# Hourglass attention and a gated FFN: pair 0's q, k and v by the hardware queues, and a new written order of the fill

## The chip, the cores and the metric

One core of a Trainium2 chip. The metric is the device time of one launch in microseconds; less is better. The core has TensorE (PE in the profile, with its weight loads as PEld), VectorE (DVE), ScalarE (ACT), GpSimd (POOL) and SyncE (SP). Each works through its own instructions strictly in the order in which they are written; DMAs are issued by SP, ACT and GpSimd.

## The reference

```python
q, k, v: (8, 8, 576, 64)          # batch, heads, positions, head width
# coarse attention on means of 4 neighbouring positions
q_d, k_d, v_d = (t.reshape(B, H, 144, 4, D).mean(axis=3) for t in (q, k, v))
out_up = repeat(softmax_attention(q_d, k_d, v_d), 4, axis=2)
# local attention: |i - j| < 4
scores = where(abs(i - j) < 4, q @ k.T / 8, -1e9)
attn_out = out_up + softmax(scores) @ v
x = attn_out.transpose(0, 2, 1, 3).reshape(4608, 512)
out = (maximum(x @ w_gate, 0) * (x @ w_val)) @ w_out       # 512 -> 1536 -> 512
```

Inputs and output are fp32; the kernel works in fp16 with fp32 sums.

## The kernel before, in words

The 64 heads are taken as 32 pairs of heads; four pairs make a batch row of 576 tokens. The FFN runs over 9 chunks of 512 tokens (`TCH`), each of 12 blocks of 128 hidden columns (`hg` products with w_gate, `hv` with w_val), and a chunk needs xT of all four pairs of its tokens. Attention runs some pairs ahead of the FFN.

Steps of a pair, with the names that the written order uses: `loadq`, `loadk`, `loadv` load q, k and v and cast them to fp16 on the way (GpSimd's queue, L328 and L358). For the first nine pairs PE turns q and k over (`tr`, L388, three groups of eight products), and `ev` copies the result from PSUM (L402), by ACT or VectorE as a letter says, the full columns to qkT and the sums of four to qkd. `s1` are the scores of both attentions (L451, L462), `ex` and `ed` their exp on ACT (L472, L486), `ma` the band mask on VectorE (L478), `vd` and `vc` the pooled v (L432, L441). For pairs 0 to 3 `su` and `sd` are the products with v (L511, L499), `ru`, `rd`, `tu`, `td` divide on VectorE, and `xp` and `xe` bring the result to xT (L646, L658). Later pairs use `den` and `num`, `ln`, `inv`, `xn` and `xsum`, and from pair 8 on the steps `scores`, `exp`, `mask`, `o`, `ln`, `xn`, `xsum` of the repeating part. From pair 9 on q and k come in halves of one head each (L333), and SP turns both over by a transposing DMA (`flip`, L368), after which VectorE pools them (`pool`, L375). From pair 11 on v is also loaded a second time (`v4`, L363), and GpSimd adds it up to vd (`v2`, L410, and `v1`, L416).

The weights come in slices: `wg`, `wv` and `wo`, four of 384 KB each, all by GpSimd's queue. The products with w_out (`p`, L748) are made in seven instead of eight parts, from sums that VectorE prepares (`wt`, L714, `next`, `sum`, L742), and SP writes the output (L698) from four y buffers.

Buffers: seven for q and k of a pair (`qk16`, pair modulo 7), seven for v, four for qkT, three for vd. A load into a buffer waits for the last reader of what was in it; for q and k of pairs 9 on that is the transposing DMA.

The order of everything is written out. The three strings are `FRONT` (the fill), `ORDER` (the repeating part) and `MAIN` (the end); each engine receives its own steps in the order of the string. A token as `qk/b2/0@1` is the third of four half loads for pair 4*1 + 2*0 + 4 + 1 + 4 = 13. In `FRONT`, `warm` and `brief` are dummy products on zeros (L833, L843), `pads` and `ones` constants that are written into buffers. Before the string the kernel issues constants and q of pair 0, which alone comes in fp32 by SP's queue and is cast by ACT (`cast`), sets constants on VectorE and runs 14 wide dummy products. GpSimd's loads carry, in the builds of both kernels, eight semaphores in turn: each waits until the load eight before it is complete.

Of the kernel before, what the change touches and what calls it, by code (L numbers as in the profile page):

```python
# [9 lines left out]
FP32 = mybir.dt.float32  # L10
# [8 lines left out]
pads loadk/0 loadv/0 loadq/1 loadk/1 loadv/1 loadq/2 cast tr/0/2/4 loadk/2 ev/0/20V/4 tr/0/1/3  # L19
tr/0/0/2 ev/0/21V/4 ev/0/10A/3 vd/0/6 loadv/2 ev/0/11A/3 ev/0/01A/2 ev/0/00A/2 loadq/3 warm/5/6  # L20
tr/1/0/7 vc/0/6 s1/0/2 ev/1/00A/7 loadk/3 tr/1/2/1 ed/0/2 tr/1/1/0 ev/1/20V/1 ev/1/11A/0 loadv/3
sd/0/6 ev/1/21V/1 ev/1/10A/0 rd/0/6 ex/0/0/2 td/0/6 wg/0 brief/16/2 vd/1/6 ev/1/01A/7 warm/2/7 ma/0/0
ex/0/1/2 s1/1/0 wv/0 ma/0/1 ed/1/0 ones/4 su/0/4 ex/1/1/0 ru/0/4 loadq/4 ex/1/0/0 tu/0/0/4
warm/5/7 tr/2/1/2 tr/2/2/3 tu/0/1/4 ev/2/11A/2 tr/2/0/0 ev/2/10A/2 loadk/4 ev/2/21V/3 xp/0/0/4 ev/2/20V/3
ev/2/01A/0 xp/0/1/5 ev/2/00A/0 ma/1/0 loadv/4 vc/1/6 warm/1/7 s1/2/0 ma/1/1 xe/0/0A/4 xe/0/1V/5 sd/1/6
ex/2/1/0 ones/5 su/1/4 rd/1/6 td/1/6 ed/2/0 ru/1/4 warm/3/7 vd/2/6 loadq/5 tu/1/1/4 ex/2/0/0 tr/3/1/2
tu/1/0/4 tr/3/2/3 loadk/5 vc/2/6 tr/3/0/0 ev/3/20V/3 ev/3/10A/2 xp/1/1/5 sd/2/6 ev/3/21V/3
loadv/5 ev/3/01A/0 xe/1/1V/5 xp/1/0/4 ev/3/00A/0 ma/2/0 ev/3/11A/2 ma/2/1 xe/1/0A/4 s1/3/0 wg/1
rd/2/6 su/2/4 td/2/6 ed/3/0 ru/2/4 ex/3/0/0 tu/2/1/4 hv/0/0/7 wv/1 hv/0/1/7 tu/2/0/4 ex/3/1/0
vd/3/6 ma/3/0 ones/6 warm/4/1 xp/2/1/5 vc/3/6 xp/2/0/4 ma/3/1 sd/3/6 xe/2/1V/5 xe/2/0A/4 loadq/6 tr/4/0/0  # L30
rd/3/6 su/3/4 td/3/6 tr/4/1/2 loadk/6 ru/3/4 hv/1/0/1 ev/4/11A/2 tu/3/0/4 hg/0/0/6 ev/4/10A/2
hg/0/1/6 tu/3/1/4 loadv/6 tr/4/2/3 ev/4/01A/0 ev/4/00A/0 xp/3/1/5 ev/4/21V/3 ev/4/20V/3 xp/3/0/4
wg/2 hv/0/2/7 xe/3/1V/5 xe/3/0A/4 hg/1/0/0 s1/4/2 wv/2 hv/0/3/7 ex/4/0/2 hv/1/1/1 loadq/7
hg/1/1/0 hg/1/2/0 ed/4/2 ma/4/0 hv/1/2/1 hg/0/2/6 hg/0/3/6 ex/4/1/2 hg/1/3/0 hv/1/3/1 relu/0/6
tr/5/0/2 ma/4/1 tr/5/1/3 loadk/7 relu/1/0 tr/5/2/4 den/4/1/5 ev/5/20V/4 vd/4/6 ev/5/10A/3
hg/3/*/0 ev/5/21V/4 gate/0/7 vc/4/6 ev/5/00A/2 gate/1/1 hg/2/*/6 ev/5/11A/3 loadv/7 ev/5/01A/2
relu/3/0 den/4/0/4 relu/2/6 hv/2/*/7 wg/3 ln/4 num/4/0/2 wv/3 gate/2/7 tr/6/1/0 inv vd/5/1
num/4/1/3 loadq/8 s1/5/4 vc/5/1 xn/2 hv/3/*/1 ex/5/0/4 ev/6/11V/0 ed/5/4 ma/5/0 hg/4/*/2
gate/3/1 ex/5/1/4 loadk/8 tr/6/0/4 relu/4/2 ma/5/1 tr/6/2/1 hg/5/*/6 ev/6/20V/1 ev/6/00A/4
ev/6/01V/4 ev/6/10A/0 ev/6/21V/1 den/5/0/4 xsum/4 wo/0 den/5/1/5 num/5/0/2 ln/4 hv/4/*/3 wo/1  # L40
inv hv/5/*/7 gate/4/3 wo/2 relu/5/6 hg/6/*/0 gate/5/7 qk/b0/0@0 num/5/1/3 relu/6/0 vd/6/1 xn/2
s1/6/4 vc/6/1 tr/7/1/0 ex/6/1/4 hv/6/*/1 ed/6/4 qk/b1/0@0 ma/6/1 hg/7/*/2 ex/6/0/4 hg/8/*/6
ma/6/0 relu/7/2 gate/6/1 qk/b2/0@0 tr/7/0/4 num/6/0/2 ev/7/01V/4 ev/7/00A/4 den/6/1/5 tr/7/2/1
qk/b3/0@0 ev/7/10A/0 den/6/0/4 ev/7/20V/1 hv/7/*/3 relu/8/6 ev/7/21V/1 xsum/5 wo/3 ln/4 hv/8/*/7
gate/7/3 inv vd/7/1 ev/7/11V/0 gate/8/7 num/6/1/3 vc/7/1 hg/9/*/0 loadv/8 xn/2 s1/7/4 relu/9/0
xsum/6 hg/10/*/2 ex/7/0/4 wt/0 v/b/0@0 ex/7/1/4 hv/10/*/3 ma/7/0 relu/10/2 ma/7/1 hv/9/*/1
ed/7/4 gate/10/3 qk/a0/1@0 hg/11/*/0 gate/9/1 qk/a1/1@0 next/0/1@0 den/7/0/4 relu/11/0 tr/8/1/2
qk/a2/1@0 den/7/1/5 flip/9 ev/8/11V/2 tr/8/2/3 ev/8/10A/2 next/1/1@0 tr/8/0/0 qk/a3/1@0
hv/11/*/1 ln/4 ev/8/01V/0 ev/8/20V/3 v/a/1@0 ev/8/21V/3 inv num/7/0/6 gate/11/1 num/7/1/7
p/1/0@1 qk/b0/1@0 ev/8/00A/0 sumhi/0/0@1 xn/6 p/2/0@1 keep/1/0@1 qk/b1/1@0 vd/8/1 xsum/7  # L50
scores/a/0@1 vc/8/1 qk/b2/1@0 sumhi/1/0@1 wt/1 vd/9/1 exp/a1/0@1 hg/0/0@1 qk/b3/1@0 ed/a/0@1
c11//0@1 v/b/1@0 sum/2/0@1 p/6/0@1 vc/9/1 relu/0/0@1 wt/2 p/5/0@1 v4/b/1@0 exp/a0/0@1 flip/10
hv/0/0@1 mask/a1/0@1 keep/2/0@1 qk/a0/0@1 mask/a0/0@1 p/7/0@1 gate/0/0@1 o/a00/0@1 sum/3/0@1
keep/3/0@1 o/a01/0@1 qk/a1/0@1 o/a10/0@1 ln/a0/0@1 o/a11/0@1 c22//0@1 hg/2/0@1 wt/3 qk/a2/0@1
ln/a1/0@1 p/3/0@1 qk/a3/0@1 pool/b/0@1 inv/a/0@1 p/4/0@1 v/a/0@1 hv/2/0@1 c21//0@1 c12//0@1
v4/a/0@1 relu/2/0@1 xn/a0/0@1 hg/1/0@1 xn/a1/0@1 hv/1/0@1 relu/1/0@1 qk/b0/0@1 flip/11
xsum/a/0@1 scores/b/0@1 gate/1/0@1 hg/3/0@1 exp/b1/0@1 qk/b1/0@1 next/0/0@1 exp/b0/0@1 qk/b2/0@1
hg/4/0@1 mask/b1/0@1 ed/b/0@1 mask/b0/0@1 qk/b3/0@1 hv/3/0@1 next/1/0@1 relu/3/0@1 gate/2/0@1
v2/b/0@1 relu/4/0@1 o/b00/0@1 o/b01/0@1 gate/3/0@1 o/b10/0@1 ln/b0/0@1 o/b11/0@1 vd/10/0
pool/a/0@1 v/b/0@1 p/1/1@1 ln/b1/0@1 hg/5/0@1 v4/b/0@1 inv/b/0@1 flip/12 hv/5/0@1 qk/a0/1@1  # L60
keep/1/1@1 xn/b1/0@1 qk/a1/1@1 p/6/1@1 xn/b0/0@1 hv/4/0@1 qk/a2/1@1 keep/2/1@1 next/2/0@1
vc/10/0 qk/a3/1@1 scores/a/1@1 relu/5/0@1 gate/4/0@1 p/7/1@1 v/a/1@1 exp/a0/1@1 gate/5/0@1
p/2/1@1 exp/a1/1@1 mask/a0/1@1 v4/a/1@1 hg/0/1@1 ed/a/1@1 mask/a1/1@1 xsum/b/0@1 keep/3/1@1
qk/b0/1@1 o/a00/1@1 relu/0/1@1 o/a01/1@1 c11//1@1 o/a10/1@1 o/a11/1@1 next/3/0@1 flip/13 p/4/1@1
ln/a1/1@1 qk/b1/1@1 pool/b/1@1 p/5/1@1 ln/a0/1@1 v2/a/1@1 hg/2/1@1 inv/a/1@1 c22//1@1 hv/0/1@1
c21//1@1 v1/a/1@1 xn/a0/1@1 hg/1/1@1 v2/b/1@1 xn/a1/1@1 p/3/1@1 relu/1/1@1 gate/0/1@1 qk/b2/1@1
scores/b/1@1 c12//1@1 hg/3/1@1 qk/b3/1@1 exp/b1/1@1 xsum/a/1@1 exp/b0/1@1 flip/14 mask/b1/1@1
qk/a0/0@2 hv/1/1@1 ed/b/1@1 mask/b0/1@1 qk/a1/0@2 hv/2/1@1 gate/1/1@1 relu/3/1@1 v4/a/0@2
pool/a/1@1 relu/2/1@1 o/b00/1@1 o/b01/1@1 o/b10/1@1 v1/b/1@1 ln/b0/1@1 o/b11/1@1 hv/3/1@1
v/b/1@1 ln/b1/1@1 hg/5/1@1 gate/3/1@1 qk/a2/0@2 inv/b/1@1 gate/2/1@1 hg/4/1@1 v1/a/0@2 xn/b1/1@1  # L70
hv/4/1@1 v4/b/1@1 relu/4/1@1 xn/b0/1@1 relu/5/1@1 qk/a3/0@2 hv/5/1@1 xsum/b/1@1 qk/b0/0@2
qk/b1/0@2 qk/b2/0@2 qk/b3/0@2 v/a/0@2
"""
MAIN = """
o:v2/a/0@6 fl/31 o:v1/b/0@6 o:v2/b/0@6 o:scores/a/0@6 o:gate/5/1@5 o:p/1/0@6 o:exp/a0/0@6 o:gate/4/1@5
o:hg/0/0@6 o:exp/a1/0@6 o:sumhi/0/0@6 o:ed/a/0@6 o:mask/a0/0@6 o:p/2/0@6 o:mask/a1/0@6 o:relu/0/0@6
o:sumhi/1/0@6 o:next/0/1@5 o:o/a10/0@6 o:keep/1/0@6 o:o/a00/0@6 o:o/a01/0@6 o:next/1/1@5 o:o/a11/0@6
# [119 lines left out]
def kernel(  # L197
# [100 lines left out]
    for t in vw[0:4]:  # L298
        nc.vector.memset(t[:, :, 64:128], 1.0)
    for t in qkT:  # L300
        nc.vector.memset(t[:, 2 * S :], 0.0)
# [887 lines left out]
```

## Time and profile before

| | |
|---|---|
| time, median of 3 runs | 344.69 us (344.06 to 345.86) |
| span of the profiled execution | 344.5 us; the page gives no other time for it |
| PE busy | 335.7 us, 97% of the span |
| DVE, ACT, POOL busy | 299.9, 238.5, 181.7 us |
| granted TensorE clock, mean | 0.995 |
| loads by GpSimd's queue | 132160 packets, 22.63 MB |

The profile is one execution. A group's row gives busy time, mean duration, idle time before it and what ended that. The timeline rows give start and duration in us. Matmuls are pipelined and their ends are modelled: a busy PE need not be a PE at its peak. A row of windows gives, for one stretch, length and mean busy time of each engine with its instructions, then the granted clock, the share of time in which the 16 DMA engines had packets under way (over 1 where they had several), and GB/s. The time of a DMA to landing is counted from its issue.

### The profile page before, as it was taken

What the parts mean: (1) busy time and instruction counts of PE and PEld (TensorE: products, weight loads), DVE (VectorE), ACT (ScalarE), POOL (GpSimd) and SP (SyncE); (2) the same over time, 40 slices, a digit from 0 to 9 for tenths busy, and PEclk for the clock granted to TensorE, in tenths of its full rate; (3) what the DMA queues carried; (4) which work ended last, traced back from release to release, by engine and by line L of the source; (5) the groups of instructions that cost most, each with busy time, mean ns of one, the idle gap of its engine ahead of it and who ended that gap; (6) DMA issues with size and microseconds to landing.
All of it is one profiled execution on the core that took longest, in us unless ns stands there. A gap on an engine that the chain in (4) does not pass through costs nothing.

```text
span 344.5 us, 8489 instructions
## 1 busy us (share of the span) xinstructions
PE 335.7 (97%) x3310; PEld 223.9 (65%) x3310; DVE 299.9 (87%) x544; ACT 238.5 (69%) x492; POOL 181.7 (53%) x232
## 2 busy tenths in 40 slices
PE   7899999999999999999999999999999999999995
PEld 3775555756565656665576657665756668888875
DVE  6495669999899999999999999999999999897692
ACT  4677876767766776677667766777776747896842
POOL 8985557677979793979378796952100000000000
PEclk9899999999999999999999999999999999999999
DMA  9999999999999999899949996993000102003014
GB/s 137 166 169 187 186 190 161 133 171 160 176 159 168 141 179 120 106 150 156 140 54 151 155 168 66 172 124 85 3 30 3 61 2 91 3 18 106 3 53 131
DMA packets 167883, 39.89 MB, mean 116 GB/s; under 512 B 149820, under 2 KB 164772, under 8 KB 167844
## 3 DMA queue, kind: packets, MB, share of 16 engines
q0 software_dynamic: 132160, 22.63, 92.6%
q1 hardware_dynamic: 35572, 16.71, 26.3%
q8 instruction: 26, 0.43, 0.6%
q14 instruction: 13, 0.11, 0.1%
q10 hardware_dynamic: 112, 0.02, 0.1%
HBM read 45.72 MB, written 9.44 MB: 160 GB/s over the span
## 4 chain that ended last, share of the span: by engine, by line
PE 89%; DVE 6%; ACT 2%; DMA 2%; issue 1%; POOL 1%; DVEq 0%; POOLq 0%
PE ps L663 42%; PE ps L909 17%; PE ps L748 15%; PE ps L609 3%; PE ps L462 2%; PE ps L451 2%; PE ps L617 2%; DMA qk<-in_q_dram 2%; PE ps L388 1%; PE ps L432 1%; DVE xT L595 1%; DVE xn L636 1%; DVE ee L478 1%; DVE qkd L375 1%; ACT ee L472 0%
## 5 line engine op out<-in xcount | busy, mean ns | idle before, releaser
L663 PE MATMUL ps<-xT,wv_sb 128*128 128x512 f16 x352 | 88.5, 379 | 0.4 <-DVE y_sb L789 0.4
L663 PE MATMUL ps<-xT,wg_sb 128*128 128x512 f16 x344 | 86.7, 379 | 0.0
L672 ACT ACTIVATE r<-ps 128x512 f16<-128x512 f32 x84 | 49.3, 596 | 28.5 <-PE ps L663 25.0
L675 DVE TENSOR_TENSOR gT<-r,ps 128x512 f16<-128x512 f16 x84 | 56.0, 679 | 5.5 <-PE ps L663 2.6
L663 PEld LDWEIGHTS <-wv_sb 128*128 128x128 f16 x352 | 32.7, 98 | 34.5 <-issue 0.6
L663 PEld LDWEIGHTS <-wg_sb 128*128 128x128 f16 x344 | 32.0, 98 | 31.2 <-issue 0.2
L636 DVE TENSOR_TENSOR xn<-ps,rden 64x720 f16<-64x720 f32 x48 | 43.5, 905 | 4.6 <-ACT rden L632 3.3
L627 ACT ACTIVATE rden<-ps 64x720 f32<-64x720 f32 x48 | 36.7, 765 | 13.4 <-PE ps L617 12.3
L472 ACT ACTIVATE ee<-ps 112x576 f16<-112x576 f32 x64 | 38.8, 648 | 6.4 <-PE ps L462 5.3
L333 POOL DMA_DIRECT2D qk<-in_k_dram x46 | 33.8, 738 | 8.0 <-DMA qk<-in_q_dram 3.5
L333 POOL DMA_DIRECT2D qk<-in_q_dram x46 | 33.7, 737 | 7.7 <-DMA qk<-in_k_dram 2.8
L478 DVE TENSOR_TENSOR ee<-ee,cst_sb 112x576 f16<-112x576 f16 x64 | 32.6, 532 | 5.3 <-ACT ee L472 4.8
L358 POOL DMA_DIRECT2D vw<-in_v_dram x30 | 28.6, 953 | 8.5 <-PE ps L388 3.7
L748 PEld LDWEIGHTS <-xo 128*128 128x128 f16 x288 | 27.3, 98 | 7.8
L375 DVE TENSOR_REDUCE qkd<-qkT 128x288 f16<-128x1152 f16 x23 | 30.9, 1343 | 0.0
L748 PE MATMUL ps<-wt,xo 128*128 128x256 f16 x216 | 27.9, 273 | 0.0
L410 POOL TENSOR_TENSOR v<-v 72x512 f32<-72x512 f16 x21 | 25.3, 1203 | 4.0 <-DMA v<-in_v_dram 3.3
L920 ACT COPY ps<-ps 128x256 f32<-128x256 f32 x54 | 19.3, 365 | 8.9 <-PE ps L909 7.6
L748 PEld LDWEIGHTS <-gT 128*128 128x128 f16 x216 | 20.8, 98 | 6.8
L595 DVE TENSOR_TENSOR xT<-xn 128x576 f16<-128x576 f16 x28 | 23.8, 850 | 0.4
L632 ACT ACTIVATE rden<-rden 128x720 f32<-128x720 f32 x28 | 22.5, 804 | 0.7
L782 ACT COPY q<-ps 128x256 f32<-128x256 f32 x36 | 13.4, 372 | 13.5 <-PE ps L748 12.8
(128 smaller groups left out, 648.4 us busy)
## 6 DMA issues: line engine op xcount, KB each, us to landing
out_dram<-y_sb SPq DMA_DIRECT2D x24, 256.0 KB, 3.1
vw<-in_v_dram POOLq DMA_DIRECT2D x30, 168.0 KB, 6.6
qk<-in_q_dram POOLq DMA_DIRECT2D x46, 72.0 KB, 6.9
qk<-in_k_dram POOLq DMA_DIRECT2D x46, 72.0 KB, 6.3
v<-in_v_dram POOLq DMA_DIRECT2D x21, 144.0 KB, 7.2
out_dram<-y_sb SPq DMA_DIRECT2D x22, 128.0 KB, 1.8
wg_sb<-in_moe_w_gate_dram POOLq DMA_DIRECT2D x4, 384.0 KB, 9.4
wv_sb<-in_moe_w_val_dram POOLq DMA_DIRECT2D x4, 384.0 KB, 10.9
```

The lines of the kernel that those rows point to most:

```text
L333: nc.gpsimd.dma_start(dst.rearrange("p (j h d) -> p j h d", h=2, d=64)[:, :, hh, :], _dap(src, off + hh * S * D, [[D, 96], [NQ * D, NB], [ ...
L358: nc.gpsimd.dma_start(t, _dap(v, base, [[D, WK], [NQ * D, n], [1, D]]))
L375: nc.vector.tensor_reduce(out=qkd[hp % 2].rearrange("p i t -> p (i t)"), in_=qkT[hp % 4][:, 0 : 2 * S].rearrange("p (t f) -> p t f", f=4), ...
L472: nc.scalar.activation(out=o, in_=ps[0:WK, p0 + 2 * g : p0 + 2 * g + 2, 0:288], func=AF.Exp, scale=scale)
L478: nc.vector.tensor_tensor(out=o, in0=o, in1=_sap(masks_sb, (0, WK), 96 * g, [[0, 2], [1, 288]]), op=ALU.mult,)
L627: nc.scalar.activation(out=rden[lo : lo + 64], in_=ps[de : de + 64, 4 + 2 * hh : 6 + 2 * hh, 0:360], func=AF.Ln)
L636: nc.vector.tensor_tensor(out=xn[lo : lo + 64], in0=ps[lo : lo + 64, 4 + 2 * hh : 6 + 2 * hh, 0:360], in1=rden[lo : lo + 64], op=ALU.mult,)
L663: nc.tensor.matmul(out=out, lhsT=w[:, kk, bass.ts(jj, 128)], rhs=xT[:, kk, c * TCH : (c + 1) * TCH], start=(kk == 0), stop=(kk == 3),)
L672: nc.scalar.activation(out=r1[j % 3], in_=h1, func=AF.Relu)
L675: nc.vector.tensor_tensor(out=gT[c % 2][:, jj, :], in0=r1[j % 3], in1=h2, op=ALU.mult)
L748: nc.tensor.matmul(out=out, lhsT=left[:, i, :], rhs=right[i], start=(first and i == 0), stop=(i == NK - 1), skip_group_check=True,)
L909: nc.tensor.matmul(out=out, lhsT=self.left[i][t], rhs=self.right[i][t], start=(i == 1 and t == 0), stop=(t == n - 1), skip_group_check=True,)
```

## The change

q, k and v of pair 0 are now all loaded in fp32 by hardware queues: q and v by SP, k by ACT. k and v go to a part of the buffer of w_out, which is loaded later. Three casts follow (`cast/q/A`, `cast/k/V`, `cast/v/A`). GpSimd begins with pair 2 and goes on with pair 1. The constants that were set in one go (`pads` and what stood before it) become single steps of the order (`pad`, `vone`, `one`). `vc` takes the engine as an argument, and is on ACT everywhere. The whole of `FRONT` is written anew: the same steps, other than these, in another order; 17 of the narrow dummy products and all 16 brief ones are gone, six pooled and one full copy more are on ACT instead of VectorE, and two xT copies more. `ORDER` and `MAIN` stay.

```diff
@@ the order of the fill (cut)
 FRONT = """
-pads loadk/0 loadv/0 loadq/1 loadk/1 loadv/1 loadq/2 cast tr/0/2/4 loadk/2 ev/0/20V/4 tr/0/1/3
...
+pad/x/1 pad/q/1 pad/x/2 vone/0 vone/1 pad/v/2 pad/e/0 pad/v/1 vone/2 pad/v/0 cast/q/A cast/k/V tr/0/1/2 tr/0/2/7
...
@@ GpSimd's own steps, in their order (loads and adds; before)
-loadk/0 loadv/0 loadq/1 loadk/1 loadv/1 loadq/2 loadk/2 loadv/2 loadq/3 loadk/3 loadv/3 wg/0 wv/0
-ones/4 loadq/4 loadk/4 loadv/4 ones/5 loadq/5 loadk/5 loadv/5 wg/1 wv/1 ones/6 loadq/6 loadk/6 loadv/6
-wg/2 wv/2 loadq/7 loadk/7 loadv/7 wg/3 wv/3 loadq/8 loadk/8 wo/0 wo/1 wo/2
-(q, k of pair 9: four halves) wo/3 (v of 8, v of 9) (pair 10: four halves, v) (pair 11: four halves, v, v4)
-(pair 12: four halves, v, v4) (pair 13: four halves) v2 of 11 ...
@@ (after)
+loadq/2 loadk/2 loadq/1 loadk/1 loadk/3 loadq/3 loadv/1 loadq/4 loadv/2 loadv/3 loadq/5 loadk/4 loadq/6
+loadk/5 wg/0 loadv/4 loadk/6 wv/0 loadk/7 loadq/7 wg/1 loadv/6 wv/1 wv/2 wg/2 loadv/7 loadv/5 loadk/8
+loadq/8 wg/3 wo/0 ones/6 wv/3 wo/1 wo/3 wo/2 loadv/8 (v of 9) (q, k of pair 9: four halves)
+(10 q, 12 q, 12 k, 10 k, 10 q, 10 k, 13 k, 11 q) (v of 10) (12 q) ones/4 (11 k, 12 k, 11 q, 13 q, 11 k)
+(v of 11) (17 k) (v4 of 13, 12, 11) (14 q, 17 k, 14 k, 16 q) (v of 12) v2 of 11 (14 k, 15 k, 13 q, 15 q)
+v2 of 12 (13 k) (15 q) v1 of 11 ...
@@ constants
-    nc.vector.memset(ones_sb[:, 0:64], 1.0)
-    nc.vector.memset(ones_sb[:, 64:128], 4.0)
-    for t in vw[0:4]:
-        nc.vector.memset(t[:, :, 64:128], 1.0)
-    for t in qkT:
-        nc.vector.memset(t[:, 2 * S :], 0.0)
-    def emit_pads(): ...
+    def emit_fill_ones(): ...
+    def emit_pad(which, i): ...        # one buffer at a time
@@ pair 0
+    first32 = wo_sb.rearrange("p k d -> p (k d)")
+    k32 = first32[0:96, 0 : 4 * NB * 64].bitcast(FP32)
+    v32 = first32[0:WK, 4 * NB * 64 : 8 * NB * 64].bitcast(FP32)
+    def emit_load_first(eng, src, dst, rows, shift):
+        b, off = head_off(0)
+        eng.dma_start(dst.rearrange("p (n d) -> p n d", d=64),
+            _dap(src, off - shift * D, [[D, rows], [NQ * D, 2 * NB], [1, D]]))
+    def emit_cast(which, eng):
+        o, i = {"q": (qk16[0][:, 0, :], q32), "k": (qk16[0][:, 1, :], k32),
+                "v": (vw[0][:, :, 0:64], v32.rearrange("p (n d) -> p n d", d=64))}[which]
+        copy_on(eng)(out=o, in_=i)
...
-        emit_load_q1(0, 0)
+        emit_load_first(nc.sync, q, q32, 96, 0)
+        emit_load_first(nc.scalar, k, k32, 96, 0)
+        emit_load_first(nc.sync, v, v32, WK, 3)
```

SP's order changes too. It was: `flip` 9 and 10, two outputs, `flip` 11, 12 and 13. It is: `flip` 9 to 12, two outputs, `flip` 13.

## The prediction

> **What bounds the kernel now.** First the page: the busy times and the chain that ended last.
>
> ```profile
> PE 335.7 (97%) x3310; PEld 223.9 (65%) x3310; DVE 299.9 (87%) x544; ACT 238.5 (69%) x492; POOL 181.7 (53%) x232
> PE 89%; DVE 6%; ACT 2%; DMA 2%; issue 1%; POOL 1%; DVEq 0%; POOLq 0%
> ```
>
> TensorE is the bound; what PE does usefully is the same in both kernels, so only time in which it waits or runs dummy products can be won, or new waits lost. Then the same by stretches (busy of PE, PEld, DVE, ACT, POOL; granted clock; DMA).
>
> ```profile
> 5.00:10.00 5.00, 4.28 (x80) 2.87 (x78) 1.68 (x9) 2.51 (x7) 5.00 (x6) 1.00 2.32 148
> 10.00:15.00 5.00, 4.17 (x62) 3.53 (x63) 1.96 (x6) 2.45 (x8) 5.00 (x7) 0.66 2.43 156
> 15.00:20.00 5.00, 4.71 (x101) 3.83 (x101) 4.60 (x13) 4.90 (x14) 5.00 (x7) 1.00 1.57 192
> 25.00:30.00 5.00, 4.97 (x71) 2.92 (x70) 3.45 (x10) 3.04 (x9) 3.44 (x5) 1.00 1.58 194
> 100.00:120.00 20.00, 20.00 (x200) 13.46 (x199) 18.56 (x31) 13.82 (x26) 16.82 (x22) 1.00 1.95 155
> ```
>
> Three things: the fill runs on latency until 15 us (clock 0.66 at 10 to 15), on ScalarE and VectorE at 15 to 25, and from about 28 PE is full; later VectorE is at 93% (18.56 of 20), so a late VectorE pushes PE at once; GpSimd issues without a pause up to 20 us and the DMA engines are loaded throughout. Last the queues: GpSimd's loads and SP's transposes by time (start, duration), and what waits for them on VectorE and PE.
>
> ```profile
> 46.17 0.73 POOL L333 DMA_DIRECT2D qk<-in_k_dram  x1 [0.35 <-DMA qk<-in_q_dram]
> 50.88 0.93 POOL L358 DMA_DIRECT2D vw<-in_v_dram  x1 [1.00 <-PE ps L663]
> 58.87 1.45 POOL L333 DMA_DIRECT2D qk<-in_k_dram  x2 [0.45 <-DMA qk<-in_q_dram]
> 72.61 1.44 POOL L333 DMA_DIRECT2D qk<-in_k_dram  x2 [1.80 <-DMA qk<-in_q_dram]
> 86.63 0.72 POOL L416 TENSOR_TENSOR vd<-v 72x256 f16<-72x256 f32 x1
> 64.63 1.30 SPq L368 DMA_TRANSPOSE qkT<-qk  x1
> 82.29 1.38 SPq L368 DMA_TRANSPOSE qkT<-qk  x1
> 102.39 1.34 DVE L375 TENSOR_REDUCE qkd<-qkT 128x288 f16<-128x1152 f16 x1
> 105.25 1.82 DVE L636 TENSOR_TENSOR xn<-ps,rden 64x720 f16<-64x720 f32 x2
> 107.58 0.25 PE L451 MATMUL ps<-qkd 64*72 64x144 f16 x2
> ```
>
> Times to landing of single windows: pair 9's last k half (46.17) 8.0, v of pair 9 (50.88) 7.4, halves at 59.5 to 61 7.2 to 7.5, at 88.5 4.9; the transposes of pairs 9, 10, 11, 13: 10.0, 7.8, 9.4, 9.2. So pair 13 is transposed at 82.29 and there at 91.5, 11 us before VectorE pools it at 102.39. This slack is what the new order of loads spends.
>
> **The change part by part.** *Pair 0.* k and v leave GpSimd (issues of 1.04 and 0.95) for ACT's and SP's queues (0.39 to 0.59 each). q, issued at 0.74 the same way, was there 3.3 us later; now three such loads and the constants share the start: bounds for q and k are 4.1 (q as before) and 6.1 (k as before by GpSimd). The 14 wide dummy products hold PE until 5.9 anyway, against 6.09 for the first transpose before: taken as zero, between +0.3 and -0.2. The casts: q as before (0.83, ACT); v 0.83 more on ACT; k on VectorE, between 0.56 (the copy of 384 columns) and twice that, hidden in the wait before VectorE's first copy at 6.54. The memsets are the same ones, some of them moved behind that point: about 1.6 us of VectorE, in gaps of 2.6 us at 7 to 10 and 12 to 15.
>
> *Dummy products.* 17 of 248 columns and 16 of 80 go; they filled waits, so their time (some 4 us) is no gain by itself.
>
> *The fill.* Pairs 0 to 3 end when the last xT copy of pair 3 does: before at 28.30 (27.90 plus 0.40). Up to there the new order puts 10 exp (0.54 apart), 5 ed (0.54), 12 full copies (0.40), 11 pooled (0.16), 5 vd (0.30), 6 xT (0.32) and 2 casts on ACT: 19.7 us against 15.4, as parts of pairs 4 to 6 come first. From 4.7 on and without a pause that ends at 24.4; at the 98% of 15 to 20 us 24.8; at the 64% of the whole fill before (15.4 of 24.2) at 35. Followed by hand with these spacings, pair 2's q is there at 7.9 (issue 1.28, behind pair 0's bytes), the first scores run at 8.2 (before 8.87), pair 0's value products at 11.7 (14.32), the scores of pair 3 at 18.1, and the last xT copy ends at 27.1, ACT 88% busy. PE has then 0.9 us more behind it (transposes of pairs 5 and 6 1.25, vd and two sums of pair 4 0.74, less five products of 0.216). Gain 28.3 - 27.1 + 0.9 = 2.1 us, between 4 and a loss.
>
> *GpSimd's queue.* The same loads in another order, and each waits until the load eight before it has landed (the builds give eight semaphores in turn). Before the last half of pair 9 now stand the whole of wo, v of pair 8 and of pair 9: the set that before was in at 50.88 + 7.4 = 58.3, against 46.17 + 8.0 = 54.2. Pair 0 by fp32 moves the same source bytes: at worst 1 us more (two loads of 1.5 instead of 1.05 and 1.15), at best 1 less (started in the idle first 2 us). So pair 9 lands at 58.3 and its transpose, 10.0 later, at 68.3: just what pooling of pair 9 (67.81) needs.
>
> *The new wait.* Pair 10's last half is issued behind pair 9's landing, 58.9, and lands 7.3 later, 66.2; transposed at 75.0 (between 74.0 and 75.6). GpSimd now has, ahead of the v loads of pairs 11 to 13, a k half of pair 17, which reuses pair 10's buffer and so waits for that transpose. GpSimd would be there at 69; it stands until 75.0. Behind it, in order: three v loads, four q/k halves (0.73 each, to 80.2); v of pair 12 waits for the k half to land (82.5); the sum of pair 11's v waits for its load (issued 77.3, plus 7.7: 85.0); then 1.15 + 4 x 0.73 + 1.15, and the last k half of pair 13 goes out at 90.2, where it was 73.3. It lands 5.2 later, 95.4, is transposed 9.2 later, 104.6, with SP's hand-over 105. VectorE stands at the pooling until then: 105 + 1.34, then the y sum 0.42, the gate 0.68 and both xn 1.82: 109.3, and PE's scores of pair 13, which need the banks that xn reads, start at 109.4 instead of 107.58: **+1.8**. These times hang on the loads, not on the fill, so the 2.1 won are lost with it. On the way vd of pair 11 ends at 92.4 (two more issues, 0.72 itself), against PE's use at 92.2: +0.2, inside the same.
>
> SP's order also changes: the transposes of pairs 11 and 12 come ahead of the first two outputs; those are 0.8 to 2.9 us of SP and have four y buffers: zero, at worst one issue, 1.7. wo waits for the casts of k and v, long done when it is issued: zero.
>
> Sum: span 344.5 + 1.8 = 346.3. The page gives no time around the span; the median 344.69 is 0.2 above, so 346.5.
>
> The Trainium skill, "DMA: Bandwidth & Descriptors", section "Issuing engines are not separate DMA queues", says that all queues end on the same 16 engines and only issue time is saved. The trace agrees as far as it goes (DMA share over 2 from 5 to 15 us); by it the stream's end at 58.3 stands and pair 0's move is worth its two GpSimd issues, 2 us, of a queue that waits for landings later.
>
> **The rivals.**
> (1) *The transposes are in time, faster.* Place: pair 13's pooling. If its transpose lands by 101, that is if GpSimd's last k half of pair 13 goes out by 86, VectorE does not wait and the fill's 2.1 stay: 342.6. For it: halves landed in 4.9 when few were under way, and after the stand at pair 17's half the queue is empty; the landings of 7.5 that I use come from crowded stretches. Against: the stand alone is 6 us.
> (2) *Given back, no more.* GpSimd 1 to 3 us earlier than worked out: pooling of pair 13 within 1.5 us of before: 344.7.
> (3) *The clock.* At 11.3 to 14.7 the granted clock was 0.5 after a stretch of 3.4 us in which PE was 64% busy. With 33 dummies fewer, PE is idle for some 1.2 us at 6.8 to 8 and 1.6 at 14.5 to 16.6. One more such stretch at 18 to 21.5 holds 3.1 us of PE work and costs 1.6 to 3.1, an early one 0.8: the 2.1 are gone and 0.3 more: 344.9 if the loads are harmless; it adds nothing to the forecast, whose wait is for loads. The Trainium skill, "TensorE: Matmul & The Clock Gate", section "What's actually happening", has this as a rule: half rate after an idle window of about 3.4 us; the trace agrees with the length of the window, but dropped at 64% busy.
> (4) *The lateness goes on, slower still.* The last k half of pair 15 goes out at 102.7, is transposed at 117, and is pooled at 119.3; 2.3 us later than that and each microsecond counts: 348.5.
>
> **How the numbers follow.** Forecast (+0.5 to +4 us around 346.5) 0.36, of which 0.30 is over 0.5% (1.7 us, what a measurement here can tell); (4) 0.18; (2) 0.16; (3) 0.08; (1) 0.22. Faster 0.22, same 0.30, slower 0.48. Range: from the whole of (1) with its bound cut at 342.6 up to 348.8; the likeliest case's own range is 345.2 to 348.0.
>
> **What would show it.** xT of pair 3 ended near 27; GpSimd idle some 6 us at 69 to 75, released by a transpose; pair 13's transpose at about 95 instead of 82.3; VectorE idle ahead of a pooling near 102 to 105, and PE idle behind it. The forecast is wrong if GpSimd passes pair 17's half without waiting, or if VectorE's pooling shows no idle time; the fill's part is wrong if granted clock falls below 1 after 15 us.

## The result, and the profile after

The changed kernel takes 355.83 us (median of 4 runs, 354.75 to 357.6), the kernel before 344.87 us beside it: 1.0327 times as long [1.0288, 1.0366], 11 us slower. The forecast of 346.5 had the direction, and its range ended at 348.8. The ratios below leave out executions that stand more than 1.5% above the fastest of the same kernel; where a kernel had such executions they are told beside it, since here they show what the clock costs.

The page of the changed kernel: busy times, granted clock in 40 slices of 8.8 us, and the chain that ended last.

```profile
PE 342.5 (97%) x3277; PEld 229.1 (65%) x3277; DVE 298.5 (85%) x536; ACT 241.0 (68%) x502; POOL 183.5 (52%) x230
...
PEclk9655799999999999999999999999999999999999
...
PE 87%; DVE 8%; DMA 2%; ACT 1%; issue 1%; DVEq 0%
```

PE is busy 6.8 us longer with 33 instructions fewer: its products take longer. The clock row says why: it is down in slices 2 to 5, about 9 to 44 us. The same stretches as were shown of before (busy of PE, PEld, DVE, ACT, POOL; granted clock; DMA), with 35 to 40 us added:

```profile
5.00:10.00 5.00, 2.08 (x30) 1.04 (x28) 1.29 (x5) 0.78 (x3) 3.99 (x5) 1.00 1.92 173
10.00:15.00 5.00, 4.62 (x79) 3.54 (x79) 3.25 (x15) 4.59 (x14) 4.00 (x5) 0.65 2.53 155
15.00:20.00 5.00, 4.96 (x75) 3.86 (x74) 4.30 (x15) 3.96 (x9) 3.97 (x5) 0.50 2.44 157
25.00:30.00 5.00, 5.00 (x67) 4.09 (x64) 3.24 (x9) 2.98 (x10) 2.82 (x4) 0.50 1.77 181
35.00:40.00 5.00, 5.00 (x46) 2.99 (x43) 0.26 (x1) 2.99 (x7) 2.59 (x4) 0.62 1.77 183
100.00:120.00 20.00, 18.84 (x167) 11.49 (x164) 19.44 (x32) 12.76 (x22) 11.88 (x15) 1.00 1.46 126
```

From 5 to 10 us PE works 2.08 us where it worked 4.28, and from 11.5 to 38.8 us it runs at half rate (granted clock 0.50), "busy" nearly all the time; before, half rate lasted from 11.2 to 14.6. The timeline of the start shows the hole (start, duration; in brackets the idle time before it and what ended it):

```profile
4.32 0.83 ACT L284 CAST qk<-q 96x768 f16<-96x768 f32 x1 [2.30 <-DMA q<-in_q_dram]
6.07 0.30 PE L353 MATMUL ps<-cst_sb,qk 96*64 96x120 f16 x4
8.34 0.56 DVE L284 CAST qk<-wo_sb 96x768 f16<-96x768 f32 x1 [3.56 <-DMA wo_sb<-in_k_dram]
8.95 0.72 PE L353 MATMUL ps<-cst_sb,qk 96*64 96x120 f16 x20 [2.59 <-DVE qk L284]
10.23 0.83 ACT L284 CAST vw<-wo_sb 112x768 f16<-112x768 f32 x1
```

q's part of the first transposes runs at 6.07, as before, but k lands at 8.3, 7.1 us after its issue at 1.19. PE waits 2.59 us for it. And the places where the forecast had its wait, on GpSimd, SP, VectorE and PE:

```profile
69.83 0.73 POOL L298 DMA_DIRECT2D qk<-in_k_dram  x1 [1.54 <-DMA qkT<-qk]
83.09 0.75 POOL L298 DMA_DIRECT2D qk<-in_k_dram  x1
90.06 1.90 SPq L333 DMA_TRANSPOSE qkT<-qk  x1
111.64 1.34 DVE L340 TENSOR_REDUCE qkd<-qkT 128x288 f16<-128x1152 f16 x1
116.48 0.25 PE L416 MATMUL ps<-qkd 64*72 64x144 f16 x2
```

GpSimd does wait at pair 17's k half for a transpose, but 1.54 us, not 6; pair 13's last half goes out at 83.09 (forecast 90.2), is transposed by an instruction that starts at 90.06, and VectorE pools it at 111.64 with no idle time ahead. That wait set nothing.

### The profile page after: what moved, and what is told of

It reads as the page before. It is cut to its first block, busy times and chain, and to the rows that moved or that the text cites. A ratio compares the mean times of both kernels' runs of the same rounds, so it can differ in the third digit from the quotient of the medians.

```text
span 352.7 us, 8411 instructions
## 1 busy us (share of the span) xinstructions
PE 342.5 (97%) x3277; PEld 229.1 (65%) x3277; DVE 298.5 (85%) x536; ACT 241.0 (68%) x502; POOL 183.5 (52%) x230
## 4 chain that ended last, share of the span: by engine, by line
PE 87%; DVE 8%; DMA 2%; ACT 1%; issue 1%; DVEq 0%
PE ps L628 39%; PE ps L874 17%; PE ps L713 14%; PE ps L574 3%; PE ps L353 3%; PE ps L427 2%; PE ps L416 2%; DVE xn L601 2%; DMA wo_sb<-in_k_dram 2%; PE ps L582 2%; PE ps L397 2%; DVE xT L560 1%; DVE gT L640 1%; DVE qkd L340 1%; PE ps L476 1%
## 5 line engine op out<-in xcount | busy, mean ns | idle before, releaser
L628 PEld LDWEIGHTS <-wv_sb 128*128 128x128 f16 x352 | 32.8, 98 | 35.4 <-issue 0.8
L592 ACT ACTIVATE rden<-ps 64x720 f32<-64x720 f32 x48 | 36.7, 765 | 12.9 <-PE ps L582 11.8
L443 DVE TENSOR_TENSOR ee<-ee,cst_sb 112x576 f16<-112x576 f16 x64 | 31.4, 505 | 10.3 <-ACT ee L437 9.2
L323 POOL DMA_DIRECT2D vw<-in_v_dram x29 | 27.5, 950 | 5.5 <-PE ps L713 2.0
L375 POOL TENSOR_TENSOR v<-v 72x512 f32<-72x512 f16 x21 | 26.6, 1266 | 5.1 <-DMA v<-in_v_dram 4.6
L381 POOL TENSOR_TENSOR vd<-v 72x256 f16<-72x256 f32 x21 | 17.7, 851 | 10.2 <-PE ps L582 10.0
## 6 DMA issues: line engine op xcount, KB each, us to landing
wg_sb<-in_moe_w_gate_dram POOLq DMA_DIRECT2D x4, 384.0 KB, 10.6
```

Of the source, the lines that this page charges most:

```text
L443: nc.vector.tensor_tensor(out=o, in0=o, in1=_sap(masks_sb, (0, WK), 96 * g, [[0, 2], [1, 288]]), op=ALU.mult,)
L592: nc.scalar.activation(out=rden[lo : lo + 64], in_=ps[de : de + 64, 4 + 2 * hh : 6 + 2 * hh, 0:360], func=AF.Ln)
L628: nc.tensor.matmul(out=out, lhsT=w[:, kk, bass.ts(jj, 128)], rhs=xT[:, kk, c * TCH : (c + 1) * TCH], start=(kk == 0), stop=(kk == 3),)
```

## The experiments

Four theories were put against each other. A: k's lateness opens the hole (PE's 2.59 us without work), the hole brings the clock down, and the half rate is nearly all of the loss. B: pair 0's lateness itself passes through. C: the new written order is what costs. D: the dummies that the new order leaves out are what held the clock.

### The hole bridged: e1_bridge

```diff
-        emit_warm(14, wide=True)
+        emit_warm(23, wide=True)
```

> The changed kernel with 23 wide dummy products ahead of the fill in place of 14, so that TensorE has work from 1.26 us to about 9 us, when pair 0's k is cast. Everything else as in the changed kernel; the first transpose still stands at about 9 us. Theory A (the 2.6 us without work at 6.4 to 9 us bring the granted clock down to 0.50, and nearly all of the loss is the 27 us at half rate): the clock stays at 1.00 past 11 us or has one dip of some 3 us as before, mean clock 0.99, time 344 to 348 us. Theory B (pair 0 is 2.9 us late, that lateness and the new order are the loss, the clock follows them): no more than 1 us less than the changed kernel, 354 to 356 us. Theory D (the dummies inside the fill that the new order leaves out are what held the clock): the clock still falls to 0.50 between 12 and 16 us and stays there, 352 us or more.

Measured: 1.0093 [1.0056, 1.0129]. Five of seven executions had a mean granted clock of 0.999 or 1.00 and took 346.0 to 348.8 us; two fell to 0.960 and 0.962, and took 356.0 and 357.9. The windows of the profiled execution, with the first product of pair 0 as late as 8.74:

```profile
10.00:15.00 5.00, 4.16 (x95) 3.24 (x95) 3.70 (x16) 4.87 (x14) 3.97 (x6) 1.00 2.64 154
15.00:20.00 5.00, 4.44 (x101) 3.66 (x98) 4.03 (x14) 5.00 (x13) 3.98 (x5) 1.00 2.44 156
```

Nine dummies, which compute nothing, take 8 us off (1.0327 to 1.0093 of 344.5) in the executions that keep the clock. Theory A holds for that share, B's bound of 1 us is broken. The two executions at 0.96 fit that the clock is the cause (some 9 us between executions of one program), and they show that bridging the hole makes the fall rarer, not impossible.

### The new order alone: e2_oldload

```diff
-        emit_load_first(nc.scalar, k, k32, 96, 0)
-        emit_load_first(nc.sync, v, v32, WK, 3)
...
-pad/x/1 ... cast/q/A cast/k/V tr/0/1/2 ... cast/v/A ...
+loadk/0 loadv/0 pad/x/1 ... cast/q/A tr/0/1/2 ...
```

> The changed kernel with pair 0's k and v loaded by GpSimd at the head of its queue as in the kernel before (q stays on SyncE's queue with its cast on ScalarE): the new written order alone. Theory A (late k): k lands at about 6 us, the first transpose is back at about 6.1 us, the clock has a dip of 3 to 7 us at most, time 343 to 348 us. Theory C (the new order of the fill, without its dummies, is itself what costs): first transpose at 6.1 us, but the clock still at 0.50 until the FFN products run without a break at 36 to 38 us, time 350 to 355 us.

Measured: 1.0037 [1.0012, 1.0062]; nine executions between 344.1 and 346.9 us at a clock of 0.995 or more, one at 0.966 and 352.4. The first transpose stands at 7.21, since the dummies, slower in this execution, ended only then; PE does not wait for k. Theory A again; what C has left is 1.3 us. So the 11 us divide, by the ratios, into 8.1 that go with the half rate, 1.9 of pair 0 by the hardware queues with the clock kept (1.0093 less 1.0037), and 1.3 of the new order; by their intervals each is known to 1 to 2 us. The profiles place the 1.9: the first transposes stand at 8.74 in the bridged run and at 7.21 here, and the 18th gate product of VectorE ends at 80.0 and 78.5. In the new order these 1.5 us of lateness go through whole.

### The dummies: e3_nodummy and e6_dummies

The kernel before without the dummies inside its fill, all 20 narrow ones (the changed kernel keeps three of them) and the 16 brief ones:

```diff
-... loadq/3 warm/5/6 tr/1/0/7 ... brief/16/2 ... warm/2/7 ... warm/5/7 ... warm/1/7 ... warm/3/7 ... warm/4/1 ...
+... loadq/3 tr/1/0/7 ...
```

> The kernel before without the dummies inside its fill (17 of 248 columns and 16 of 80 left out; the 14 wide ones ahead of the fill stay). Theory D (the dummies hold the clock): at 0.50 from about 10 us to about 30 us, time 351 to 354 us. Theory A (only a gap of over 2 us without work brings it down for long): the first transpose stays at 6.1 us, the clock has one dip of 3 to 7 us, time 343.5 to 346.5 us.

Measured: 1.0037 [1.0005, 1.0069]; four of ten executions with the clock at 0.999 or 1.00 (344.6 to 346.0 us), four at 0.98 (346.0 to 347.3), and two at 0.97 (351.1 and 355.5). The profiled one is of the middle kind:

```profile
10.00:15.00 5.00, 3.60 (x63) 3.04 (x59) 3.22 (x9) 3.80 (x9) 5.00 (x7) 0.61 2.43 157
15.00:20.00 5.00, 4.87 (x71) 3.94 (x69) 3.57 (x11) 3.56 (x10) 4.61 (x7) 0.50 1.59 190
20.00:25.00 5.00, 5.00 (x72) 3.97 (x71) 3.25 (x10) 3.24 (x9) 3.84 (x5) 0.52 2.40 158
```

Half rate lasts from 11.1 to 24.8 us here, against 3.4 us with the dummies, though PE waits no longer than 0.94 us at once ahead of it. The fall needs no late load, and the dummies are what keep it short. Of 87 executions of the kernel before that were run beside the first fourteen experiments, none had a mean clock under 0.993.

The changed kernel with the hole not bridged and 14 dummies more at 13 us:

```diff
-... ex/0/1/3 warm/1/3 ev/2/01A/7 pad/e/1 warm/1/4 vc/0/A/1 ...
+... ex/0/1/3 warm/8/3 ev/2/01A/7 pad/e/1 warm/8/4 vc/0/A/1 ...
```

> The changed kernel with two of its own dummies made longer (1 of 248 columns to 8, twice, at about 12.4 us); the gap at 6.4 to 9 us stays. Theory D2 (the gap starts the half rate, and the dense dummies that the new order leaves out are what ended it after 3.3 us in the kernel before): clock back at 1.00 by 16 to 20 us, mean clock 0.98 or more, some 4 us of dummies at half rate paid, 15 to 20 us of half rate saved, time 347 to 352 us. If dummies don't end it: still 0.50 until 38 us or later, 358 to 360 us.

Measured: 1.018 [1.0134, 1.0227], all four executions at a clock of 0.988 to 0.995.

```profile
10.00:15.00 5.00, 4.69 (x48) 3.54 (x48) 2.89 (x11) 3.33 (x8) 3.71 (x5) 0.51 2.51 155
15.00:20.00 5.00, 4.72 (x93) 3.67 (x90) 2.37 (x10) 2.92 (x9) 3.94 (x5) 0.81 2.43 157
25.00:30.00 5.00, 5.00 (x118) 4.23 (x116) 4.65 (x15) 4.67 (x14) 2.52 (x4) 1.00 1.77 185
```

Full rate is back at 16.9, after 6.8 us, in place of 38.8, and 5 us are saved although the dummies themselves take time. The hole differs between executions: all begin the wide dummies at 1.26, but 14 of them end anywhere from 5.9 to 7.4 us, since their first part runs at half rate and full rate comes at 4.1 to 7.2. In this profiled execution the hole was 1.52 us, and the clock fell all the same, at 10.1. So D is half right: what made 3 us into 27 is that nothing dense stands in the fill any more. That the hole opens the stretch in the changed kernel the bridge shows as a matter of how often, four of four executions against two of seven: a hole is not needed (the run above), and one of 1.5 us ended in a fall here and in none with k on SP (below).

### Why k is late, and pair 0 alone: e4_hwload, e5_ksp, e7_ksp_old, e8_vgp

Only pair 0's sources changed, in the old order with its dummies:

```diff
-        emit_load_q1(0, 0)
+        emit_load_first(nc.sync, q, q32, 96, 0)
+        emit_load_first(nc.scalar, k, k32, 96, 0)
+        emit_load_first(nc.sync, v, v32, WK, 3)
...
-pads loadk/0 loadv/0 loadq/1 ... loadq/2 cast tr/0/2/4 ... vd/0/6 ...
+pads loadq/1 ... loadq/2 cast/q/A cast/k/V tr/0/2/4 ... cast/v/A vd/0/6 ...
```

> The kernel before with pair 0 alone changed: q and v in fp32 by SyncE's queue, k by ScalarE's, casts of q and v on ScalarE and of k on VectorE, GpSimd beginning with pair 1; the old written order and its dummies stay. Theory A (late k): first transpose at 8.7 to 9.1 us, a gap of 2.5 us on TensorE, clock down to 0.50 from 11 us for 3 to 20 us, time 347 to 353 us. If the dummies of the old order bring the clock back quickly (theory D), 346 to 348 us: the 2.9 us of lateness less what later pairs make up. If pair 0's source costs nothing, 344.5 us.

Measured: 1.0169 [1.0109, 1.0228] over three executions (clock 0.995, 0.995 and 0.98; the fourth, at 0.981, took 353.7). First transpose at 8.47, half rate from 10.6 to 14.0. This part alone, in an order that shortens the fall, costs 6 us, and 3.8 and 5.5 in the two executions at 0.995. Its lateness is not made up: PE waits once more, for ScalarE's cast of v,

```profile
10.38 0.60 PE L451 MATMUL ps<-vw,cst_sb 112*128 112x128 f16 x6 [1.09 <-ACT vw L337]
```

and the second gate product ends at 36.5 us against 33.6 in the profile of before, which had a fall of the same length; the 84th still ends 3.4 us later.

The changed kernel, and then this old order, with k behind q on SP and v on ACT:

```diff
-        emit_load_first(nc.scalar, k, k32, 96, 0)
-        emit_load_first(nc.sync, v, v32, WK, 3)
+        emit_load_first(nc.sync, k, k32, 96, 0)
+        emit_load_first(nc.scalar, v, v32, WK, 3)
```

> The changed kernel with two sources exchanged: k of pair 0 stands on SyncE's queue right behind q, v of pair 0 on ScalarE's queue. Nothing else moves, no dummy is added. Theory A (k late on ScalarE's queue opens the gap, the gap brings the clock down): k lands at 5 to 6.5 us, first transpose at 5.7 to 7 us, no gap of over 1 us, clock at 1.00 in most executions, time 344 to 347 us; pair 0's v then lands at 7 to 8.5 us. If k is late because all three loads share the DMA engines (theory S), k lands at 7 us or later on either queue, first transpose at 7.7 us or later, and the clock and 350 us or more remain.

> The kernel before with pair 0 by the hardware queues, as in the run of that part alone, but k behind q on SyncE's queue and v on ScalarE's. Theory A: first transpose at 5.7 to 7 us, 343.5 to 345.5 us: the 4 to 6 us that the part alone lost with k on ScalarE's queue are gone. Theory S (all loads share the DMA engines and k comes at 7 us or later): 347 us or more.

Measured: 1.01 [1.007, 1.0129] in the new order and 1.0155 [1.0096, 1.0214] in the old one. k's cast stands at 7.46 and 7.24, the first product that needs k at 8.07 and 8.08: k comes about 0.9 us earlier than in the changed kernel (8.34) and 0.6 earlier than with k on ACT in the old order (7.86), not 2. That is what the theory of shared engines gave for k, against my expectation of 5 to 6.5; the 350 us that it gave for the new order were not reached. In the profiled execution of the new order the hole is 1.57 us and the clock stays at 1.00; two others had 0.98. In the old order three of four had 0.985 or less; one of them, at 353.0 us, is not in the ratio.

The changed kernel with only v given back to GpSimd:

```diff
-        emit_load_first(nc.sync, v, v32, WK, 3)
...
-pad/x/1 ... cast/v/A ...
+loadv/0 pad/x/1 ...
```

> The changed kernel with only pair 0's v given back to GpSimd (first in its queue, direct to f16); q stays on SyncE's queue, k on ScalarE's. Theory S (336 KB of v beside it are what delays k): k lands 1.5 us or more earlier, at 6.8 us or before, first transpose at 7.5 us or before. If ScalarE's queue itself is slow for these 1152 runs of 256 bytes (theory Q): k lands at 7.8 to 8.3 us again, first transpose at 8.5 to 9 us, gap and half rate as in the changed kernel, 353 to 357 us.

Measured: 1.0025 [0.9968, 1.0081], clock 0.99 to 1.00; in the profiled execution the hole is 0.88 us, and half rate still lasts from 9.7 to 16.5. DMA issues from 0 to 12 us in this run (KB, us from issue to landing), then in the run with k on SP:

```profile
wo_sb<-in_k_dram ACTq DMA_DIRECT2D x1, 288.0 KB, 5.8
```

```profile
wo_sb<-in_v_dram ACTq DMA_DIRECT2D x1, 336.0 KB, 7.3
q<-in_q_dram SPq DMA_DIRECT2D x1, 288.0 KB, 3.8
wo_sb<-in_k_dram SPq DMA_DIRECT2D x1, 288.0 KB, 6.2
```

k takes 5.8 us with v out of the way, 6.2 behind q on SP, 7.1 in the changed kernel: it is neither ScalarE's queue nor one neighbour alone. q, issued 0.4 us ahead of the others, still takes 3.6 and 3.8 us with all three (3.3 before); the loads behind it are the late ones, and none of these ways has k at the 6.1 us at which GpSimd's load had it. Giving v back undoes nearly all of the loss. Whether by the earlier k or by the cast of v that ScalarE no longer does (0.83 us, at 10.2), the run doesn't tell apart.

### Lateness alone: e13_late

```diff
 (kernel before)
-        emit_warm(14, wide=True)
+        emit_warm(22, wide=True)
```

> The kernel before with 22 wide dummies ahead of the fill in place of 14, and nothing else changed: the first transpose at 8.5 to 8.9 us in place of 6.1, all queues as before. If a late start of pair 0 passes through to the end: 346 to 347 us, clock at 1.00. If later waits take it up (pair 1's loads at 8.5 to 9.2 us, VectorE and ScalarE full at 15 to 25 us): 344.3 to 345 us.

Measured: 1.0021 [0.9999, 1.0043], every execution at a clock of 0.999 or 1.00. The dummies ended sooner than I meant:

```profile
7.78 0.82 PE L388 MATMUL ps<-cst_sb,qk 96*64 96x120 f16 x24
```

Pair 0 is 1.7 us late, and 0.7 us or so (0.2%) is left of it at the end, if anything. In the old order theory B has little as long as the clock holds and only the start is late: it is mostly made up. The new order and the hardware loads in the old one did not make it up (above).

### Where the new order's own gain went: e9 to e12, e14, e15

The new order is ahead and then is not. The 18th and 24th gate products of VectorE end at 78.5 and 95.4 us in the run of the new order alone, against 82.2 and 99.1 before; the 30th ends at 119.7 against 119.4. The profile of before had half rate in its fill; an execution of the old order without it (that of the last run below) has 80.5 and 98.2, so the order's own lead is 2.0 to 2.8 us. Between, VectorE's instructions in the run of the new order alone and GpSimd's beside them:

```profile
103.35 1.36 DVE L560 TENSOR_TENSOR xT<-xn 128x576 f16<-128x576 f16 x1
104.64 1.50 DVE L707 TENSOR_TENSOR xo<-gT 128x768 f16<-128x768 f16 x1
106.06 2.22 DVE L443 TENSOR_TENSOR ee<-ee,cst_sb 112x576 f16<-112x576 f16 x1
```

```profile
104.11 1.60 POOL L375 TENSOR_TENSOR v<-v 72x512 f32<-72x512 f16 x1
...
106.14 0.72 POOL L381 TENSOR_TENSOR vd<-v 72x256 f16<-72x256 f32 x1
106.83 1.14 POOL L375 TENSOR_TENSOR v<-v 72x512 f32<-72x512 f16 x1
```

Undisturbed these three take 0.74, 0.54 and 0.45 us. PE then waits 1.55 and 1.06 us for the masked `ee`. In this execution, of mean clock 0.995, half rate from 109.4 to 112.8 follows that idle time and takes part of the lead too; eight of the nine executions in the ratio had 0.998 or more. Theory G: they stretch because GpSimd adds at the same time. The Trainium skill, "SBUF — State Buffer", section "SBUF: two separate sides", has it as a rule: the two engines share a pair of SBUF ports under an exclusive lock that one instruction holds to its end, and a VectorE instruction with two SBUF inputs needs it against a GpSimd instruction that reads SBUF. The next run agrees: without the adds the three instructions take 0.74, 0.54 and 0.45 us again. The lock alone does not give the first length, though: the xT product begins 0.76 us ahead of the add that is shown beside it. The run is the new order alone without the two adds of 104.1 and 106.8 (the first-step sums of v of pairs 14 and 15, whose pooled v is then not complete):

```diff
-        if NVP <= hp < NP:
+        if NVP <= hp < NP and hp not in (14, 15):
             t, m = v4[hp % NV4], v2[hp % 2]
```

> The run of the new written order with pair 0's k and v by GpSimd, with the first-step sums of v of pairs 14 and 15 left out (so the pooled v of these two pairs is not the reference's): the two adds that stood beside VectorE's stretched products at 104 to 108 us. Theory G: VectorE's xT, xo and ee instructions at 103 to 109 us take 0.45 to 0.76 us each in place of 1.36 to 2.22, TensorE idles under 0.7 us there in place of 2.6, pooling of pair 14 at 107 to 108 in place of 110.3. If VectorE's long instructions are not GpSimd's doing: they stay at 1.4 to 2.2 us and the idle time stays at 2.6 us.

```profile
103.57 0.74 DVE L560 TENSOR_TENSOR xT<-xn 128x576 f16<-128x576 f16 x1
104.23 0.54 DVE L707 TENSOR_TENSOR xo<-gT 128x768 f16<-128x768 f16 x1
104.70 0.45 DVE L443 TENSOR_TENSOR ee<-ee,cst_sb 112x576 f16<-112x576 f16 x1
```

Measured: 0.9965 [0.9937, 0.9993], 342.9 us, 2.5 under the same order with the adds (1.0037); PE has no idle time from 100 to 120 us. The same two adds left out of the kernel before:

> The kernel before with the same two adds left out, the first-step sums of v of pairs 14 and 15 (so the pooled v of these two pairs is not the reference's). If the adds hurt the new order alone because they meet VectorE's fp16 products there (theory G), the kernel before, whose adds at 103.4 and 105.3 us stand beside instructions that read PSUM, gains under 0.7 us: 344 to 344.8 us. If their own work or their place costs in any order (theory W): 342 to 343 us, as in the new order.

Measured: 1.0008 [0.9982, 1.0033]. There the same adds cost nothing. So it is not their work but what they meet: in the new order VectorE is some 4 us further along when GpSimd comes to them. In the profile of before they run at 103.4 and 105.3, the second beside xn, which reads PSUM and takes its usual 1.82 us.

Three attempts to have the gain with the adds complete. First, in the new order alone, GpSimd's wait of 4.0 us for a load taken out of the way:

```diff
-... v2/b/0@1 ... v2/a/1@1 ...
+... v2/b/0@1 v2/a/1@1 ...
```

> The run of the new written order with pair 0's k and v by GpSimd, and in GpSimd's order one more edit: the first step of the 4:1 sums of v (for pair 11), which there waited 4.0 us at 76.2 to 80.2 for a load, stands behind the four loads of q and k that followed it. Theory G (the new order is 3.7 us ahead up to pair 13's pooling at 98.7, and loses it at 104 to 111 because GpSimd, late by that wait, does its two-input adds beside VectorE's fp16 products, which then take 1.4 to 2.2 us in place of 0.5 to 0.75): GpSimd's adds of 104.1 and 106.8 come 3 to 4 us earlier, the stretched VectorE instructions there are gone or fewer, TensorE's 2.6 us of idle time at 108 to 110 falls under 1 us, time 342 to 344 us, 1.5 to 3 us under the 345.5 of that run. Theory L (GpSimd's loads or something later sets the pace from pair 16 on, and the lead is lost in any case): pooling of pair 17 and the later pairs stays at 138 us and on as in the kernel before, time 344.5 to 346 us.

Measured: 1.0017 [0.9989, 1.0046]; one of twelve executions at 0.966 and 352.7. The adds came at 103.8 and 106.1, hardly earlier, because GpSimd then waited 2.4 us for a load of v at 102. In the profiled execution only one instruction there was stretched (1.18 us), PE did not wait, and it was among the fastest. Then the same edit in the changed kernel with v by GpSimd and six dummies more:

> The changed kernel with pair 0's v given back to GpSimd, 20 wide dummies ahead of the fill in place of 14 (to reach k's cast at about 8 us), and the same add moved behind four loads. Theories A and G together: clock at 1.00 in most executions, first transpose at about 8 us, no stretched VectorE instructions at 101 to 108 us, time 342.5 to 344.5 us, at or under the kernel before. If the lead can't be kept past pair 16 (theory L): 345 to 347 us.

Measured: 1.0059 [1.0036, 1.0083]; one of twelve at 0.964 and 351.7. And the adds put behind four loads instead, in the new order alone and in the bridged kernel:

```diff
+            if base == PS // 4:
+                for t in ("v2/b/0", "v1/a/1", "v2/a/0"):
+                    toks.remove(t)
+                    toks.insert(toks.index("v4/a/1"), t)
```

> The run of the new written order with pair 0's k and v by GpSimd, with nothing left out: the sum of v of pair 15 (two adds) and the first add of pair 14, at 104 to 108 us there, stand behind the three loads of q and k and the one of v that followed them. Theory G: VectorE's instructions at 103 to 107 us take 0.45 to 0.76 us, the adds stand at about 108 to 111 us beside products that read PSUM, TensorE idles under 1 us at 100 to 112 us, time 342.3 to 344 us, up to 2.6 us under the 345.5 of that run. If the adds' own work on GpSimd is what costs, wherever it stands (theory W): 345 to 346 us.

> The changed kernel with its gap bridged by 23 wide dummies, and the same three adds behind the four loads. Theory G: 345 to 346 us where the clock holds, 1.5 to 2.6 us under the 347.5 of the bridged run; the rest over the kernel before is pair 0's lateness. Theory W: 347 to 348 us.

Measured: 1.0001 [0.9972, 1.003] (two of twelve executions at 0.966, 352.6 and 353.2) and 1.0089 [1.0054, 1.0124] (three of ten at 0.960 to 0.964, 356.5 to 359.2). Theory G's ranges were missed; the second result lies where theory W had it, though the old order without the adds speaks against W. The instructions at 104 to 106 us are short again, but others are met. One line of the first run, one of the second:

```profile
113.70 1.50 DVE L707 TENSOR_TENSOR xo<-gT,xo 128x768 f16<-128x768 f16 x1
```

```profile
108.78 2.37 DVE L443 TENSOR_TENSOR ee<-ee,cst_sb 112x576 f16<-112x576 f16 x1 [0.15 <-ACT ee L437]
```

By these single profiles, moving the adds moves the meeting. No complete kernel here is measurably faster than the one before; the new order with the old loads and the shifted adds equals it in time, with a clock that sometimes falls.

## Why the prediction was right or wrong

Three steps failed: k's landing was taken as no later than before, the dummy products were priced at nothing, and the loss of clock was left out of the sum. The wait that was in the sum did not occur.

**Pair 0.** This is the step that failed first. It took q and k at 4.1 to 6.1 us and the first transpose as unchanged, between +0.3 and -0.2. q kept to it (cast at 4.32); k's cast stood at 8.34 and the transposes waited 2.59 us. The upper bound was the landing of another load by another queue, not that of the third fp32 load beside two of its size. The same part's figure for v's cast, 0.83 us, was met.

**Dummy products.** "No gain by itself" named what they filled and not what they held. Their price is the second term that was missing: without them half rate lasted 13.7 us in the old order (3.4 with them), and 27 us in the new one.

**The clock (rival 3).** The mechanism that decided was written down and priced at one or two stretches of 3.4 us, 0.8 to 3.1 us, with a chance of 0.08. Two things in it were wrong: that it comes in single stretches, and that it adds nothing to the forecast. It lasted from 11.5 to 38.8 us, and 8 of the 11 us go with it. The Trainium skill, "TensorE: Matmul & The Clock Gate", section "What's actually happening", has full rate back after one busy window of about 3.4 us. Here PE showed as busy without a break from 20 to 38 us at half rate and the clock did not rise; products of 248 columns brought it back 4 us after the first of them (13.0 to 16.9 in the run with 14 more). The measurement decides: a busy row of the profile was not enough.

What sorts the stretches can be worked out from the 17 profiles of this case. In all of them the granted clock, after its first change, changes only at whole multiples of 3.41 us. For each such stretch take the work of the array: every product's columns, times the share of the 128x128 array that its weights fill, added up and divided by the columns that a stretch could take at full rate. (512 columns take 0.43 us at half rate and 0.22 at full, as the wide dummies show; so these make 0.50 at half rate.)

| run, stretch in us, granted clock | PE busy | work | clock after it |
|---|---|---|---|
| before, 7.8 to 11.2, full | 0.66 | 0.32 | half |
| changed, 8.1 to 11.5, full | 0.54 | 0.30 | half |
| k on SP, 8.4 to 11.8, full | 0.67 | 0.37 | full |
| changed, 14.9 to 18.3, half | 1.00 | 0.31 | half |
| changed, 35.4 to 38.8, half | 1.00 | 0.41 | full |
| 14 dummies more, 13.5 to 16.9, half | 1.00 | 0.46 | full |

The nine full-rate stretches ahead of a fall had a work of 0.19 to 0.34, all others at full rate 0.37 or more. At half rate the 20 that stayed there had 0.27 to 0.37, the 26 that rose 0.36 or more. PE's busy share does not sort them: it was 0.36 to 0.69 ahead of a fall, and as low as 0.49 without one. At half rate even the wide dummies make only 0.50, so products that fill under 0.7 of the array stay below 0.36 without any pause; the transposes fill 0.38. This is read from the profiles afterwards and no run tested it; records that are missing can shift a figure by some hundredths. By it the hole, the late k and the missing dummies are one cause: too little work in a stretch of 3.41 us.

The free-running window of the Trainium skill (the same section) would fit that one program falls in some executions and not in others: in seven of the kernels some executions had a mean clock under 0.975 and others 0.99 or more.

**The fill.** Its mechanism was right and is hidden by the clock: the last xT copy of pair 3, forecast to end at 27.1 and at 36.5 in the changed kernel, ends at 27.4 in the run of the new order alone. The lead is 3.7 us over the profile of before at the 18th and 24th gate products, but 2.0 and 2.8 over an execution of the old order whose clock held: close to the 2.1 forecast.

**GpSimd's queue and the new wait.** The place was right, the size was not: 1.5 us at pair 17's half in place of 6, and 1.8 with the clock kept. GpSimd passes it at 69.8, so pair 10's transpose was done by then, not at 75.0. The terms that were off: the last half of pair 10, issued at 58.88 as forecast, landed 3.2 us later and not 7.3, and its transpose took 7.1 and not 8.8. In the run of the new order alone pair 13's last half goes out at 85.7, not 90.2, and the pooling at 98.7 has no idle time ahead of it. The +1.8 of the sum did not occur, so that the forecast had the direction was luck.

**Rival 1** set its own condition, last half out by 86: it was met in that run, and still the gain was not kept. The step that failed there is "then VectorE does not wait, and the fill's 2.1 stay": VectorE did not wait, it was stretched by GpSimd's adds, a cost for which neither the forecast nor a rival had a term. Without the two adds that order takes 342.9, near the rival's 342.6. **Rival 2** (given back) has about the right figure for the new order alone, 344.7 against 345.3, by another cause: luck. **Rival 4** needed the same wait as the forecast and falls with it.

**The sum's base.** I set the time 0.2 above the span, from a span and a median of different executions. Executions that give both have the time about 1.8 above the span (344.33 beside 342.5), and the profiled execution of before, with a half-rate stretch, was slower than most. The two errors cancel: the 346.5 is the median before plus the 1.8 of the wait, and this base was right by luck.

What stays open: why the old order makes up a late start by dummies (0.7 us left of 1.7) and not one by the hardware loads. The profile shows PE's wait for ScalarE's cast of v and a fall in the second; no run takes either away alone.

## What to carry to other kernels

Before dummy products are taken out, or a first load is moved, ask what TensorE does in the first 10 us in the worst case of that load's landing, and look at the granted clock over the whole of the latency-bound stretch: bridging a hole of 2.6 us won 8 us, and 14 cheap dense products later in the fill won 5. Count the work of the array in each 3.4 us there, not how busy TensorE is shown. Measure how long a load takes among the neighbours that the change gives it, not as it was measured alone. When an engine gets ahead, look whom it meets: VectorE 4 us further along ran into GpSimd's adds and lost 2.5 us by them.

## What the runs showed of the hardware that I had not expected

- Half rate went on for 27 us with PE shown as busy throughout, and ended with dense products (clock 0.50 from 15 to 30 us, busy 4.96 and 5.00 of 5). The work of the array in a stretch of 3.41 us, not the busy share, told what the clock did next: 0.34 or less in every stretch ahead of a fall, 0.37 or more in every other stretch at full rate.
- Executions of one program differ by 5 to 11 us with the mean granted clock alone: 346.0 to 348.8 us at 0.999 to 1.00 against 356.0 and 357.9 at 0.96 in the bridged kernel.
- Two GpSimd adds of 1.15 us cost 2.5 us of the whole program in one order and nothing in another; a VectorE product of 0.45 us took up to 2.37.
- An fp32 load of 288 KB landed 3.3 us after its issue when it was alone on the hardware queues beside the constants, 3.6 to 3.8 us as the first of two or three, and 5.8 to 7.1 us when it was issued 0.4 us or so behind another of its size.
